# Query-state product over four array tiles, and a written engine order for the first sixteen steps

## The chip, the core and the metric

The kernel runs on one core of one Trainium2 chip. The core has a matrix engine (TensorE, PE in the profile; the loads of its stationary operand are PEld), VectorE (DVE), ScalarE (ACT), GpSimd (POOL) and a queue engine that issues transfers (SP). The metric is the device time of one launch in microseconds (us).

## The reference

Three layers in a row. The first is a delta-rule attention with batch 4, 8 heads, 768 tokens and head size 48; the second a dense two-layer net (384 to 2048 to 384, leaky relu) on the 3072 resulting tokens; the third a layer of 8 experts (384 to 1024 to 384, relu) in which each token goes to one expert.

```
k_n = k / (norm(k) + 1e-6)
for t in range(768):                      # per batch and head
    y[t] = q[t] @ state                   # state: 48 x 48
    state += beta[t] * outer(k_n[t], v[t] - k_n[t] @ state)
h = y @ w_in;  x = max(0.01 * h, h) @ w_out
e = argmax(x @ w_gate)                    # expert of the token
out = prob * sigmoid(x @ w_output_gate)[e] * (relu(x @ w1[e]) @ w2[e])
```

## The kernel before

The 768 tokens are cut into 12 chunks of 64 (`NCH`, `CH`). The 32 batch-head pairs are held 2 x 16: a slot 0 to 15 in the free dimension, and one of the two halves of the partitions (0 to 63, 64 to 127). In a chunk the recurrence is solved with matmuls. The gram of the keys (`gram`, L73) gives a 64 x 64 matrix per head; its diagonal 32 x 32 blocks are copied out (`k_gram_out`, L104, into `td`), transposed, scaled by key norms and beta (`norms`, L169) and inverted row by row (`inverse`, L218), for two chunks, a pair, at a time. `flipped` (L239) transposes the inverse and `z_make` (L254) copies it to z. Pair 0 is inverted on VectorE, every later pair on GpSimd.

`chain` (L298) is a generator that computes one chunk in sections, one for each step: the right side from v and the old state (L339), `solve` with z, with the off-diagonal block lx, and with z again (L316), the state update (L373 to L379), and the result y. y is the sum of two products, both written by `read` (L321, matmul at L323): the query-state product (`state_part`, L347: queries of the chunk times old state) and the masked query-key product ap times the solved u (L384 to L386). `take` (L308) copies the solved columns out of the accumulation banks ks, one half on ScalarE, one on VectorE. y goes to xx as two float16 parts.

The array takes 64 x 64 tiles: the row half follows from the partitions of the operands, the column half from the partitions of the output. In `state_part` before, head half `ab` has operands and output at the same half:

```
        for m in range(GM):
            for g in parts:
                for ab in gs:
                    k.mark_y = read(g, ab, m, old_w, GM * (g ^ ab) + m, half(ab, 48), t.q, m == 0, False)
```

while the product of ap with u runs over `ALL4`, that is over all four pairs of row half and column half. The call `state_part((1,))` is put off (`k.between`) behind the expert product of the third section's step, `state_part((0,))` behind that of the next.

The dense net runs in steps: 8 for each chunk, `moe1_up` (L508, products L518, relu L525 to L532) and `moe1_down` (L536) of one eighth of the 2048 columns. Its weights come as float32 and are made into two float16 parts by `conv` (L450): three VectorE passes (L459 to L461), two ScalarE copies (L466, L467) and a GpSimd subtraction (L468) for each of 24 blocks of 512 columns. Expert weights are converted in the same way in the background from step 16 on (`back`, L481) and stored to DRAM.

`weave` (L947) sets the order. It loads and prepares pair 0, then runs steps n = 0 to 15: chunk 0's and 1's chains, two conversions per step for n below 8 and one for n from 8 to 15, the dense net of chunk 0 from n = 8, and the generator `prepare(1)` (L949), which makes pair 1's inverse. Up to step 16 a scheduler orders the instructions of each engine, within the given program order, priorities and a few written edges (`issue_after`). From step 16 on (L1104) the order of PE, DVE and ACT is the written one. Accumulation banks are drawn from rings: psA and psS (two buffers each, psS for grams, query products and y), psL (two, for the dense net's products and the conversions) and psO (psO0, psO1, for its sums). `moe1_setup` (L409) loads gate weights and constants; its casts are L415, L416 and L420. The transposes and tables of the expert layer come after the last chunk and are not edited.

Of the kernel before, what the change touches and what calls it, by code (L numbers as in the profile page):

```python
# [86 lines left out]
def k_gram(k, c, td):  # L87
    ga = gram_banks(k, c)
    gram(k, ga, k.chunks[c].kc, k.chunks[c].kc, ALL4)
    k_gram_out(k, c, td, ga)  # L90
# [13 lines left out]
def k_gram_out(k, c, td, ga):  # L104
    V, A = k.nc.vector, k.nc.scalar
    for ab in range(2):
        for s, dst, src in td_blocks(c, td, ga, ab):
            if c < 2 and s:
                k.mark_tv = V.tensor_copy(dst, src)
            else:  # L110
                k.mark_td = A.activation(dst, src, AF.Copy)
    for ab in range(2):
        lx_out(k, c, ga, ab)
# [55 lines left out]
def norms(k, w, td):  # L169
    nc = k.nc  # L170
    V, G = nc.vector, nc.gpsimd
    E = V if w == 0 else G
# [14 lines left out]
    for i in range(3):  # L187
        E.tensor_tensor(z, y, y, op=ALU.mult)
        if w:
            E.tensor_tensor(z, z, n2, op=ALU.mult)  # L190
            E.tensor_scalar(z, z, -0.5, 1.5, op0=ALU.mult, op1=ALU.add)
            E.tensor_tensor(y, z, y, op=ALU.mult)
        else:
            V.scalar_tensor_tensor(z, z, -0.5, n2, op0=ALU.mult, op1=ALU.mult)
            V.scalar_tensor_tensor(y, z, 1.5, y, op0=ALU.add, op1=ALU.mult)
    E.tensor_tensor(y, y, n2, op=ALU.mult)
    E.tensor_scalar(y, y, 1e-6, None, op0=ALU.add)
    V.reciprocal(z, y)
    E.tensor_tensor(z, z, z, op=ALU.mult)
    E.tensor_tensor(z, z, k.beta[:, w], op=ALU.mult)  # L200
    E.tensor_scalar(n2, z, -1.0, None, op0=ALU.mult)
    E.tensor_tensor(x, x, n2.unsqueeze(1).to_broadcast([128, 32, 32]), op=ALU.mult)
    if w:
        E.affine_select(x, x, pattern=[[1, 32], [-1, 32]], compare_op=ALU.is_gt, fill=0.0, base=0, channel_multiplier=0)
    E.memset(xf[:, 0:1024:33], 1.0)
    V.transpose(s.nw, y)
    return s
# [63 lines left out]
def q_products(k, c):  # L271
# [4 lines left out]

    def mask():
        for ab in range(2):
            k.nc.vector.tensor_tensor(t.ap[:, GM * ab : GM * ab + GM], gq[ab], k.amask[:, ab : ab + 1].to_broadcast([128, GM, 64]), op=ALU.mult)
# [18 lines left out]
def chain(k, c):  # L298
# [9 lines left out]
    def take(dst, scale):  # L308
        k.mark_uh = A.activation(dst[:, ms[0]], ks[0], AF.Copy, scale=scale)  # L309
        k.mark_u = V.tensor_scalar(dst[:, ms[1]], ks[1], scale, None, op0=ALU.mult)  # L310
# [30 lines left out]
    yield  # L341
    solve(t.z, r, 0, 0, True)
    take(u, 1.0)
    yield
    y = []

    def state_part(parts):  # L347
        if not y:
            y.extend(banks())
        for m in range(GM):  # L350
            for g in parts:
                for ab in gs:
                    k.mark_y = read(g, ab, m, old_w, GM * (g ^ ab) + m, half(ab, 48), t.q, m == 0, False)
# [55 lines left out]
def moe1_setup(k):  # L409
    nc, sb = k.nc, k.const  # L410
    V, A, G = nc.vector, nc.scalar, nc.gpsimd
    k.wg = [sb.tile([128, 3, 16], F16, name=f"wg{h}") for h in range(2)]
    wg32 = sb.tile([128, 3, 16], F32, name="wg32")
    nc.sync.dma_start(wg32, k.wg_d.rearrange("p (a e) -> p a e", a=3))
    A.activation(k.wg[0], wg32, AF.Copy, scale=1024.0)  # L415
    V.scalar_tensor_tensor(k.wg[1], wg32, 1024.0, k.wg[0], op0=ALU.mult, op1=ALU.subtract)  # L416
# [3 lines left out]
    V.tensor_copy(k.cmat, cst)  # L420
# [5 lines left out]
    V.tensor_copy(k.run, k.base)  # L426
# [5 lines left out]
    nc.sync.dma_start(k.xd[DUM : DUM + 1, :], dum)  # L432

# [5 lines left out]
def conv_load(k, pool, n):  # L439
# [4 lines left out]
    else:  # L444
        raw = pool.tile([128, 1024], I32, tag="w64", name=f"w64_{n}")
# [4 lines left out]
def conv(k, pool, n):  # L450
    nc = k.nc
    V, A, G = nc.vector, nc.scalar, nc.gpsimd
    i, which = n // 2, n % 2
    dst, sc = ((k.win, 1024.0), (k.wout, 2048.0))[which]
    w64 = k.w64.pop(n)
    ps, tag = (k.psO, f"psO{n // 2 % 2}") if n < 8 and n % 2 else (k.psL, "psL")
    wt = ps.tile([128, 512], I32, tag=tag, name=f"wt_{n}")
    lo, hi = w64[:, :, 0], w64[:, :, 1]
    V.tensor_scalar(wt, hi, 5, 2, op0=ALU.logical_shift_left, op1=ALU.logical_shift_right)  # L459
    V.scalar_tensor_tensor(wt, hi, -0x40000000, wt, op0=ALU.bitwise_and, op1=ALU.bitwise_or)  # L460
    V.scalar_tensor_tensor(wt, lo, 29, wt, op0=ALU.logical_shift_right, op1=ALU.bitwise_or)  # L461
    w32 = wt.bitcast(F32)
    cs = slice(512 * i, 512 * i + 512)
    h, l = (columns(d)[:, cs] for d in dst)
    ws = pool.tile([128, 512], F32, tag="wt", name=f"ws_{n}")
    A.activation(ws, w32, AF.Copy, scale=sc)  # L466
    A.activation(h, ws, AF.Copy)  # L467
    G.tensor_tensor(l, ws, h, op=ALU.subtract)  # L468
# [478 lines left out]
def weave(k):  # L947
    nc = k.nc
    def prepare(w):  # L949
        a, b = 2 * w, 2 * w + 1  # L950
        td = k.xp.tile([128, 32, 32], F32, tag="xx", name=f"td{w}")
        yield
        yield
        k_gram(k, a, td)
        yield
        yield
        yield
        k_gram(k, b, td)
        yield
        yield  # L960
        with k.tc.high_priority():
            s = norms(k, w, td)
        yield
        for i in range(6):
            inverse(k, w, s, CUTS[i], CUTS[i + 1])
            if i == 5:
                nv_load(k, a)
            yield
        done = k.after
        with k.tc.issue_after(done.ins):  # L970
            nv_make(k, a, s)
        nv_load(k, b)
        yield
        with k.tc.issue_after(done.ins):
            nv_make(k, b, s)
        with k.tc.issue_after(k.mark_gl.ins) if hasattr(k, "mark_gl") else ExitStack():
            flipped(k, w, s)
        z_make(k, a, s)
        yield
        z_make(k, b, s)  # L980

# [11 lines left out]
    k_load(k, 2)  # L993
    q_load(k, 0)
    nv_load(k, 0)
    es = ExitStack()
    wst = es.enter_context(k.tc.tile_pool(name="wst", bufs=2))
    conv_load(k, wst, 0)
    conv_load(k, wst, 1)
    nconv, nback = 0, 0  # L1000
    td = k.p1.tile([128, 32, 32], F32, tag="td", name="td0")
    for c in range(2):
        ga = gram_banks(k, c)
        for s in range(2):
            gram(k, ga, k.chunks[c].kc, k.chunks[c].kc, ((0, s), (1, s)))
        k_gram_out(k, c, td, ga)
    mark_td = k.mark_td
    s0 = norms(k, 0, td)
    masked_scale(k, s0)
    nv_make(k, 0, s0)  # L1010
    inverse(k, 0, s0, 1, 31)
    moe1_setup(k)
    ch = chain(k, 0)
    run(ch)
    run(ch)
    z_make(k, 0, s0, True)
    after = k.after
    turn = nc.gpsimd.tensor_copy(k.const.tile([128, 1], F32, name="turn"), k.z[0][:, 15, 31:32])

    def convert():  # L1020
        nonlocal nconv, es
        if nconv < 24:
            conv(k, wst, nconv)
            ahead = nconv + (10 if nconv < 2 else 6 if nconv < 12 else 2)
            if (nconv < 2 or nconv >= 6) and not 12 <= nconv < 16 and ahead < 24:
                conv_load(k, wst, ahead)
            nconv += 1
            if nconv == 24:
                es.close()
                k.bg = k.late.enter_context(k.tc.tile_pool(name="bg", bufs=6))  # L1030

    k_load(k, 3)
    kg_load(k, 0)
    nv_load(k, 1)
    for n in range(2, 10):
        conv_load(k, wst, n)
    pg = prepare(1)
    hold = ExitStack()
    for m in (mark_td, turn, after):
        hold.enter_context(k.tc.issue_after(m.ins))  # L1040
    for _ in range(4):
        run(pg)
    q_gram(k, 0)
# [345 lines left out]
```

## Time and profile before

| | us |
|---|---|
| median of 3 runs (849.51 to 851.61) | 850.45 |
| the profiled execution, its own time | 855.32 |
| its span, first to last instruction | 853.4 |
| PE busy in the span | 768.0 |
| DVE, ACT, POOL busy in the span | 483.4, 328.6, 414.4 |

The profile is of one execution. An engine is busy while an instruction of it runs; matmuls overlap, so the busy time of a group of them is the union of their spans, and a mean duration is longer than the pace at which they follow. Idle time in brackets stands ahead of an instruction, with what ended it. The granted clock (PEclk) is a share of 2.4 GHz: 0.50 is the lower of its two levels, 1.00 the upper.

### The profile page before, as it was taken

To read this page: it belongs to the slowest core of one execution; us is meant where nothing else is said; L and a number is where in the kernel's file an instruction comes from. 1 tells how busy PE (TensorE), PEld (TensorE's weight loads), DVE (VectorE), ACT (ScalarE), POOL (GpSimd) and SP (SyncE) were. 2 spreads that over 40 slices of the span, in tenths; PEclk is the share of its full clock that TensorE was granted. 3 is DMA by queue.
4 is the path that set the end of the run, shared out by engine and by line. 5 is a ranking of instruction groups with operands and counts; after the bars stand their busy time and mean duration, and the time that the engine had idled before them with its cause. 6 is when DMAs were issued, how large, how long until landed. Compare 5 with 4: busy or idle time off the path is not lost. (4 is left out here: it accounts for less than half of the span.)

```text
span 853.4 us, 29444 instructions
## 1 busy us (share of the span) xinstructions
PE 768.0 (90%) x12642; PEld 591.4 (69%) x12642; DVE 483.4 (57%) x1109; ACT 328.6 (39%) x650; POOL 414.4 (49%) x590
## 2 busy tenths in 40 slices
PE   4044898999999999999999999999997999999993
PEld 4044676777777777777777777777775778778782
DVE  2999784766666566657666767775362222222230
ACT  2246546434644464445534465543311111111110
POOL 0017995688468846884588526521132221222110
PEclk7555799999999999999999999999998999999997
DMA  8714434724662458244724397948726537898440
GB/s 265 269 51 148 153 108 142 183 82 142 194 205 71 138 183 228 73 139 144 216 81 139 121 271 214 319 142 323 326 69 221 84 85 214 223 337 232 134 115 13
DMA packets 100137, 145.03 MB, mean 170 GB/s; under 512 B 42320, under 2 KB 69747, under 8 KB 97186
## 3 DMA queue, kind: packets, MB, share of 16 engines
q1 hardware_dynamic: 94882, 128.10, 49.5%
q0 software_dynamic: 5120, 15.00, 5.7%
q8 instruction: 101, 1.65, 0.8%
q14 instruction: 34, 0.28, 0.1%
HBM read 152.28 MB, written 35.42 MB: 220 GB/s over the span
## 5 line engine op out<-in xcount | busy, mean ns | idle before, releaser
L518 PE MATMUL h<-xx,win 128*128 128x256 f16 x1728 | 207.1, 275 | 1.4 <-ACT ws L466 1.4
L543 PE MATMUL o<-wout,gh 128*128 128x384 f16 x768 | 186.0, 326 | 0.7 <-ACT u L309 0.6
L518 PEld LDWEIGHTS <-win 128*128 128x128 f16 x1728 | 164.5, 98 | 27.7 <-issue 1.4
L543 PE MATMUL o<-wout,gl 128*128 128x384 f16 x384 | 123.6, 326 | 2.5 <-DVE gl L532 2.5
L888 PEld LDWEIGHTS <-wb 128*128 128x128 f16 x2016 | 115.7, 98 | 4.8 <-issue 1.4
L528 DVE SCALAR_TENSOR_TENSOR h<-h,g 128x512 f32<-128x512 f32 x96 | 66.7, 695 | 72.1 <-ACT g L525 67.8
L525 ACT ACTIVATE g<-h 128x512 f32<-128x512 f32 x96 | 57.3, 597 | 122.6 <-PE h L518 114.2
L888 PE MATMUL hp<-xT,wb 128*128 128x128 f16 x1728 | 100.9, 220 | 0.0
L892 DVE SCALAR_TENSOR_TENSOR h<-hp,h 128x512 f16<-128x512 f32 x48 | 33.2, 692 | 118.8 <-ACT h L891 108.8
L543 PEld LDWEIGHTS <-gh 128*128 128x128 f16 x768 | 70.8, 98 | 42.7 <-issue 0.8
L491 POOL TENSOR_SCALAR we<-we 128x512 f32<-128x512 f32 x35 | 52.8, 1510 | 97.8 <-ACT whl L487 78.2
L532 DVE TENSOR_TENSOR gl<-h,gh 128x512 f16<-128x512 f32 x96 | 66.3, 690 | 58.1 <-ACT gh L529 56.9
L902 PE MATMUL o<-wb,h 128*128 128x384 f16 x576 | 97.4, 326 | 0.0
L908 POOL DMA_INDIRECT out_dram<-y,row x24 | 23.9, 998 | 141.5 <-DVE y L907 135.5
L529 ACT ACTIVATE gh<-h 128x512 f16<-128x512 f32 x96 | 57.3, 597 | 85.6 <-DVE h L528 85.5
L891 ACT ACTIVATE h<-hp 128x512 f16<-128x512 f32 x48 | 28.7, 597 | 157.8 <-PE hp L888 157.8
L232 POOL TENSOR_TENSOR x<-x,tmp 128x30 f32<-128x30 f32 (+9 forms) x150 | 81.3, 542 | 11.2
L230 POOL TENSOR_TENSOR tmp<-x 128x30 f32<-128x30 f32 (+9 forms) x150 | 77.9, 519 | 10.8
L902 PEld LDWEIGHTS <-h 128*128 128x128 f16 x576 | 55.3, 98 | 34.4
L487 ACT ACTIVATE whl<-we 128x512 f16<-128x512 f32 x96 | 56.6, 623 | 6.8 <-DMA we<-in_we_dram 3.5
L316 PE MATMUL ks<-r,z 32*32 32x48 f32 x1536 | 27.6, 212 | 35.0 <-DVE z L259 28.2
L494 DVE SCALAR_TENSOR_TENSOR whl<-we,whl 128x512 f16<-128x512 f32 x61 | 51.9, 869 | 10.9 <-ACT whl L487 9.2
(253 smaller groups left out, 1018.3 us busy)
## 6 DMA issues: line engine op xcount, KB each, us to landing
wb<-wd SPq DMA_DIRECT2D x56, 1536.0 KB
we<-in_we_dram SPq DMA_DIRECT2D x96, 256.0 KB
wd<-whl SPq DMA_DIRECT2D x96, 256.0 KB
kc<-in_kt_dram SPq DMA_DIRECT2D x24, 224.0 KB
q<-in_qt_dram SPq DMA_DIRECT2D x24, 224.0 KB
nv<-in_kv_dram SPq DMA_DIRECT2D x12, 384.0 KB
kn<-in_kv_dram SPq DMA_DIRECT2D x12, 384.0 KB
w<-in_win_dram SPq DMA_DIRECT2D x6, 512.0 KB
```

The lines of the kernel that those rows point to most:

```text
L230: E.tensor_tensor(tv, x[:, q, j : j + 1].to_broadcast([128, n, j]), x[:, j : j + 1, 0:j].to_broadcast([128, n, j]), op=ALU.mult)
L232: k.after = E.tensor_tensor(x[:, q, 0:j], x[:, q, 0:j], tv, op=ALU.add)
L487: nc.scalar.activation(hl[:, 0], w32, AF.Copy, scale=sc)
L491: nc.gpsimd.tensor_scalar(w32, w32, sc, None, op0=ALU.mult)
L518: PE.matmul(hp[:, ff], k.win[l][:, f, kk], xx[:, r, kk], start=(n == 0), stop=(n == 8))
L525: A.activation(g32, hp, AF.Copy, scale=0.01 * 2.0**-10)
L528: V.scalar_tensor_tensor(hp, hp, 2.0**-10, g32, op0=ALU.mult, op1=ALU.max)
L529: k.mark = A.activation(gh, hp, AF.Copy)
L532: k.mark_gl = V.tensor_tensor(gl, hp, gh, op=ALU.subtract)
L543: k.mark_down = k.nc.tensor.matmul(k.o[t], gg[l][:, ff, 128 * t : 128 * t + 128], k.wout[r][:, f], start=(f == 0 and i == 0), stop=(f == N ...
L888: PE.matmul(hp[:, ff], w1[:, l, kk, 128 * f : 128 * f + 128], t.xT[:, 3 * r + kk], start=(i == 0), stop=(i == 8))
L902: nc.tensor.matmul(o, t.h[l][:, f], w2[:, r, f], start=(i == 0), stop=(i == 23))
```

## The change

Half of the heads (those in slots with `b1` = 1) get their keys, queries and state at the other partition half than their result: `layout_attention` permutes them on the host, and `read` takes the column half p and the rows separately. Four consecutive calls of `state_part` then go over both row halves and both column halves, and its two calls move: for odd chunks the first is put behind the expert product of the step of the first solve, for even chunks it stands in the chain ahead of the lx solve; the second always follows the second z solve.

Up to step 16 all four engines follow a written order now. Copies of the grams of chunks 0 and 1 come ahead of the casts of constants; `moe1_setup` is split into loads (`moe1_loads`), casts, and `gate_weights` in step 14. The grams of chunks 2 and 3 are written before pair 0's inverse. Loads are issued in another order. Conversions become a stream of single passes (`Conv`): `take` and the end of the sections call `k.fill`, which writes the next ones; 7 blocks come before the first expert product, the others in the eight steps of chunk 0. For the first six blocks the low part is made by TensorE: a bank is opened with an identity product, VectorE writes the value into it, and a product with a negated scaled identity subtracts the high part. Pair 1's inverse is cut by rows: 12 after chunk 0, then three in each step.

```
 def gram_banks(k, c):
-    ps, tags = (k.psO, ("psO0", "psO1")) if c in (1, 2) else (k.psS, ("psS", "psS"))
+    ps, tags = (k.psO, ("psO0", "psO1")) if c in (1, 3) else (k.psL, ("psL", "psL")) if c == 2 else (k.psS, ("psS", "psS"))
...
     def take(dst, scale):
+        k.fill()
         k.mark_uh = A.activation(dst[:, ms[0]], ks[0], AF.Copy, scale=scale)
...
-    def read(g, ab, m, w, f, p, right, clear, last):
+    def read(g, p, m, w, f, rows, right, clear, last):
         cols = 64 if c == 0 or w is old_w else 48
-        return PE.matmul(y[g][half(ab, cols), m % NPR, m // NPR], w[p, f * D : f * D + cols], right[p, f], start=clear, stop=last, skip_group_check=True)
+        return PE.matmul(y[g][half(p, cols), m % NPR, m // NPR], w[rows, f * D : f * D + cols], right[rows, f], start=clear, stop=last, skip_group_check=True)
...
+    def state_part(part):
+        if not y:
+            y.extend(banks())
+        for i in range(NPR):
+            for b in gs:
+                g, m = b ^ 1 ^ part, NPR * b + i
+                for p in gs:
+                    read(g, p, m, old_w, GM * (g ^ p) + m, half(p ^ b, 48), t.q, part == 0 and i == 0, False)
+
     solve(t.z, r, 0, 0, True)
     take(u, 1.0)
+    if c > 1 and c % 2:
+        k.between.append(lambda: state_part(0))
     yield
...
+    if c > 1 and c % 2 == 0:
+        state_part(0)
     solve(t.lx, u, 0, 1, False)
     take(r, -1.0)
-    if c > 1:
-        k.between.append(lambda: state_part((1,)))
     yield
     if c == 1:
-        state_part(gs)
-    with k.tc.issue_after(k.mark_y.ins) if c == 1 else ExitStack():
-        solve(t.z, r, 1, 1, True)
+        state_part(0)
+    solve(t.z, r, 1, 1, True)
     if c > 1:
-        k.between.append(lambda: state_part((0,)))
+        k.between.append(lambda: state_part(1))
     take(u, 1.0)
     yield
...
                 f = GM * ab + m
                 PE.matmul(ks[s][half(ab, 48), m], t.kg[half(s), f], u[half(s), f], start=True, stop=True, skip_group_check=True)
+        k.fill()
+        if c == 1:
+            state_part(1)
...
         for ab, s in ALL4:
-            read(s ^ ab, ab, m, u_w, GM * ab + m, half(s), t.ap, c == 0, True)
+            p = ab ^ (m // NPR)
+            read(s ^ p, p, m, u_w, GM * ab + m, half(s), t.ap, c == 0, True)
+    k.fill()
...
+def conv_bank(k, ps, tag, name):
+    wt = ps.tile([128, 512], I32, tag=tag, name=name)
+    k.nc.tensor.matmul(wt.bitcast(F32), k.ident, k.ident.unsqueeze(1).to_broadcast([128, 4, 128]), start=True, stop=True)
+    return wt
...
+    def low(self):
+        if self.bank is not None:
+            self.k.nc.tensor.matmul(self.w32, self.k.minus[:, self.n % 2], self.h, start=False, stop=True, skip_group_check=True)
+            self.k.nc.scalar.activation(self.l, self.w32, AF.Copy, scale=self.sc)
...
+    nv_load(k, 0)
+    wg32, cst = moe1_loads(k)
     q_load(k, 0)
-    nv_load(k, 0)
+    k_load(k, 3)
...
+    order = es.enter_context(k.tc.manual_schedule(engines={E.PE, E.DVE, E.Activation, E.Pool}))
...
+    ga = k_gram(k, 3)
+    k_gram_out(k, 3, td, ga)
+    banks = [conv_bank(k, k.psO, f"psO{i}", f"wb{i}") for i in range(2)] + [conv_bank(k, k.psL, "psL", f"wc{i}") for i in range(2)]
+    inverse(k, 0, s0, 1, 31)
     z_make(k, 0, s0, True)
...
+    fills += [
+        [lambda: pair.update({1: norms_first(k, 1, td)}), vec],
+        [mask, vec],
+        [vec, vec],
+        [lambda: norms_second(k, 1, pair[1]), vec],
+        [vec],
+    ]
...
+    for n in range(8, 16):
+        s = n - 8
         down, up = up, None
...
+        moe1_up(k, 0, s, (lambda: ops(BEFORE[s]), lambda: ops(1)))
+        up = (0, s, k.gg)
+        sca()
+        inv(1)
+        for _ in range(AFTER[s]):
+            ops(3)
+            sca()
+        if s == 0:
+            q_products(k, 1)()
+        if s < 6:
+            run(ch)
...
+        sca()
+        inv(2)
...
         if s == 7:
-            ch = chain(k, p + 1)
+            ch = chain(k, 2)
             run(ch)
...
+            ga = k_gram(k, 4)
+            k_gram_out(k, 4, td, ga)
+            flipped(k, 1, pair[1])
+            z_make(k, 2, pair[1])
+            z_make(k, 3, pair[1])
...
+EARLY = 6
+BEFORE = (2, 2, 2, 2, 2, 2, 2, 2)
+HOMES = "010101010SSLLLLLLLAAAALL"
+AFTER = (1, 2, 2, 2, 1, 1, 1, 0)
...
     for s, h, ab, b1, pr in np.ndindex(2, 2, 2, 2, NPR):
-        at = 2 * (s ^ ab) + b1, 2 * pr + ab
+        p = ab ^ b1
+        at = 2 * (s ^ p) + b1, 2 * pr + p
```

## Rows read from the trace of the kernel before

**Rows 1.** Busy time by stage: start:end, length, busy (instructions) per engine, clock, DMA.
```profile
core 0: us, PE busy (x) PEld busy (x) DVE busy (x) ACT busy (x) POOL busy (x), PEclk, DMA share, GB/s
27.00:50.00 23.00, 0.00 (x0) 0.00 (x0) 22.58 (x119) 2.86 (x9) 1.19 (x1) 0.50 0.48 151
50.00:92.00 42.00, 23.09 (x594) 20.55 (x595) 41.86 (x71) 26.43 (x51) 25.37 (x37) 0.54 0.39 134
92.00:135.00 43.00, 43.00 (x722) 31.02 (x722) 30.55 (x48) 22.55 (x42) 39.39 (x66) 0.94 0.33 107
...
150.00:350.00 200.00, 197.84 (x3804) 149.86 (x3805) 131.44 (x284) 96.34 (x202) 143.25 (x233) 1.00 0.52 152
350.00:558.00 208.00, 205.98 (x3887) 155.30 (x3880) 139.76 (x283) 104.56 (x204) 134.45 (x176) 1.00 0.61 181
```

**Rows 2.** Busy time by stage, two stretches of 10 us, same columns.
```profile
80.00:90.00 10.00, 6.34 (x166) 5.78 (x164) 9.96 (x20) 5.26 (x9) 8.44 (x14) 0.50 0.51 173
130.00:140.00 10.00, 7.72 (x163) 5.88 (x161) 3.07 (x5) 4.35 (x11) 7.23 (x14) 1.00 0.41 137
```

**Rows 3.** Timeline, 0 to 51 us: start, length, engine, line, out<-in [idle before <-releaser].
```profile
3.82 5.38 PE L77 MATMUL ga<-kc 48*64 48x64 f32 x128 [3.82 <-DMA kc<-in_kt_dram]
...
15.76 0.24 ACT L415 ACTIVATE wg<-wg 128x48 f16<-128x48 f32 x1 [5.62 <-DMA wg<-in_wg_dram]
...
17.27 1.76 DVE L109 COPY td<-ga 32x256 f32<-32x256 f32 x4
...
19.07 1.25 DVE L180 STREAM_TRANSPOSE x<-td 128x1024 f32<-128x1024 f32 x1
...
23.99 1.03 DVE L332 SCALAR_TENSOR_TENSOR ks<-nv,nw 128x384 f32<-128x384 f32 x2
...
27.13 1.07 DVE L230 TENSOR_TENSOR tmp<-x 128x14 f32<-128x14 f32 x1
...
49.91 0.37 DVE L259 COPY z<-zt 128x256 f32<-128x256 f32 x1
...
50.34 2.47 PE L316 MATMUL ks<-r,z 32*32 32x48 f32 x64 [28.23 <-DVE z L259]
```

**Rows 4.** Timeline, 80 to 165 us, TensorE and VectorE.
```profile
91.76 4.00 PE L518 MATMUL h<-xx,win 128*128 128x256 f16 x18 [1.41 <-ACT ws L466]
...
135.26 2.14 PE L518 MATMUL h<-xx,win 128*128 128x256 f16 x18
...
138.13 1.25 DVE L241 STREAM_TRANSPOSE zt<-x 128x1024 f32<-128x1024 f32 x1 [5.05 <-POOL x L234]
...
142.97 0.88 PE L316 MATMUL ks<-r,z 32*32 32x48 f32 x64 [1.17 <-ACT r L309]
...
149.00 0.88 PE L316 MATMUL ks<-u,lx 32*32 32x48 f32 x64
...
152.47 1.15 PE L323 MATMUL y<-q,state 48*64 48x64 f32 x32 [0.51 <-ACT td L120]
```

**Rows 5.** Groups by line, 50 to 135 us: busy, mean ns | idle before, releaser.
```profile
L459 DVE TENSOR_SCALAR wt<-w 128x512 int32<-128x512 int32 x12 | 8.2, 689 | 1.0 <-ACT ws L466 0.9
L528 DVE SCALAR_TENSOR_TENSOR h<-h,g 128x512 f32<-128x512 f32 x8 | 5.6, 696 | 4.6 <-ACT g L525 4.6
...
L468 POOL TENSOR_TENSOR win<-ws,win 128x512 f16<-128x512 f32 x12 | 13.9, 1157 | 14.3 <-ACT win L467 14.3
```

**Rows 6.** Timeline of TensorE: both products of y, each with the instruction behind it.
```profile
117.65 1.10 PE L323 MATMUL y<-ap,u 64*48 64x64 f32 x60
118.68 2.14 PE L518 MATMUL h<-xx,win 128*128 128x256 f16 x18
...
158.49 1.15 PE L323 MATMUL y<-q,state 48*64 48x64 f32 x32
159.57 0.50 PE L543 MATMUL o<-wout,gh 128*128 128x384 f16 x2
```

More of the change, by code (lines that the diff above doesn't have):

```diff
@@ L169, in norms @@
 def norms(k, w, td):
[L170 to L172 removed]
+    V = k.nc.vector
     s = Ctx()
@@ L444, in conv_load @@
     else:
-        raw = pool.tile([128, 1024], I32, tag="w64", name=f"w64_{n}")
+        raw = pool.tile([128, 1024], I32, tag="w64", bufs=3, name=f"w64_{n}")
     k.nc.sync.dma_start(raw, (k.win_d, k.wout_d)[which][i].bitcast(I32))
     k.w64[n] = raw.rearrange("p (a b) -> p a b", b=2)
[L450 to L468, printed above, removed]
@@ L948, in weave @@
     nc = k.nc
[L949 to L980, printed above, removed]
     def run(g):
@@ new lines, in weave, with fill, stream @@
+    q_load(k, 1)
+    for n in range(6, 10):
+        conv_load(k, k.wst, n)
+    kg_load(k, 1)
+    nback = 0
+    E = mybir.EngineType
+    order = es.enter_context(k.tc.manual_schedule(engines={E.PE, E.DVE, E.Activation, E.Pool}))
+    ready, fills = [], []
+    def fill():
+        for f in fills.pop(0) if fills else ():
+            f()
+    k.fill = fill
+    def stream():
+        homes = dict(zip("01SLA", ((k.psO, "psO0"), (k.psO, "psO1"), (k.psS, "psS"), (k.psL, "psL"), (k.psA, "psA"))))
+        for n, home in zip(ORDER, HOMES):
+            u = Conv(k, n, banks[n % 4] if n < EARLY else None, homes[home])
+            for _ in u.vector():
+                yield
+            ready.append(u)
+            yield
@@ L1001, in weave, with ops, vec, inv @@
+    late = []
+    todo = stream()
+    def ops(n):
+        for _ in range(n):
+            next(todo, None)
+    def vec():
+        ops(3)
+    rows = iter(range(1, 31))
+    def inv(n):
+        for j in [j for _, j in zip(range(n), rows)]:
+            inverse(k, 1, pair[1], j, j + 1)
+    def sca():
+        for u in ready:
+            u.scalar()
+            late.append(u)
+        ready.clear()
+    def low():
+        for u in late:
+            u.low()
+        late.clear()
     td = k.p1.tile([128, 32, 32], F32, tag="td", name="td0")
+    gas = []
@@ L1002, in weave @@
     for c in range(2):
-        ga = gram_banks(k, c)
+        gas.append(gram_banks(k, c))
         for s in range(2):
-            gram(k, ga, k.chunks[c].kc, k.chunks[c].kc, ((0, s), (1, s)))
-        k_gram_out(k, c, td, ga)
-    mark_td = k.mark_td
-    s0 = norms(k, 0, td)
+            gram(k, gas[c], k.chunks[c].kc, k.chunks[c].kc, ((0, s), (1, s)))
+    for c in range(2):
+        td_out(k, c, td, gas[c])
+    for c in range(2):
+        for ab in range(2):
+            lx_out(k, c, gas[c], ab)
@@ L1009, in weave @@
+    s0 = norms(k, 0, td)
+    nc.scalar.activation(k.cmat, cst, AF.Copy)
+    nc.scalar.activation(k.wg[0], wg32, AF.Copy, scale=1024.0)
+    k.minus = k.const.tile([128, 2, 128], F16, name="minus")
+    for w in range(2):
+        nc.scalar.activation(k.minus[:, w], k.ident, AF.Copy, scale=-(2.0 ** -(10 + w)))
+    ga = k_gram(k, 2)
     masked_scale(k, s0)
+    td = k.p1.tile([128, 32, 32], F32, tag="td", name="td1")
+    k_gram_out(k, 2, td, ga)
     nv_make(k, 0, s0)
-    inverse(k, 0, s0, 1, 31)
@@ L1012, in weave @@
-    moe1_setup(k)
+    nv_make(k, 1, s0)
     ch = chain(k, 0)
@@ L1015, in weave @@
     run(ch)
-    z_make(k, 0, s0, True)
[L1017 to L1043, printed above, removed]
[L1044 to L1070 removed]
+    mask = q_products(k, 0)
@@ new lines, in weave @@
+    run(ch)
+    sca()
+    run(ch)
+    low()
+    sca()
+    z_make(k, 1, s0)
+    run(ch)
+    low()
+    sca()
+    run(ch)
+    low()
+    sca()
+    run(ch)
+    low()
+    sca()
+    inv(12)
+    ch = chain(k, 1)
+    run(ch)
+    low()
+    banks.clear()
+    ops(3)
+    run(ch)
+    sca()
+    up = down = tail = None
+    for n in range(8, 16):
+        s = n - 8
+        down, up = up, None
+        moe1_up(k, 0, s, (lambda: ops(BEFORE[s]), lambda: ops(1)))
+        up = (0, s, k.gg)
+        sca()
+        inv(1)
+        for _ in range(AFTER[s]):
+            ops(3)
+            sca()
+        if s == 0:
+            q_products(k, 1)()
+        if s < 6:
+            run(ch)
+        if s == 5:
+            k_load(k, 5)
+        sca()
+        inv(2)
@@ L1082, in weave @@
+            z_make(k, 2, pair[1])
+            z_make(k, 3, pair[1])
+        if s == 1:
+            k_load(k, 4)
+        if s in (2, 3):
+            nv_load(k, s)
+            nv_make(k, s, pair[1])
+        if s == 3:
+            q_load(k, 2)
+        if s == 5:
+            kg_load(k, 2)
+        if s == 6:
+            gate_weights(k, wg32)
         if down is not None:
             moe1_down(k, *down)
-            if down[1] == 7:
-                tail = moe1_tail(k, down[0], k.o)
-        with k.tc.issue_after(k.mark_down.ins) if down is not None else ExitStack():
-            if n and n not in (1, 3, 15):
-                run(pg)
-            if n == 12:
-                td = k.p1.tile([128, 32, 32], F32, tag="td", name="td2")
-            if n == 13:
-                k_load(k, 5)
@@ L1093, in weave @@
-    hold.close()
+    es.close()
+    k.bg = k.late.enter_context(k.tc.tile_pool(name="bg", bufs=6))
     for n in range(AHEAD):
```

157 lines of the change are left out of this document (80 added, 77 removed).

## The prediction

> **What bounds the kernel now.** I began with the busy time by stage [rows 1]. From 150 to 558 us TensorE is busy 403.8 of 408 us at full clock: there, whatever shortens TensorE's list shortens the kernel. From 92 to 135 it is busy throughout, but up to 92 it is not the bound: no matmul from 27 to 50, 23.1 of 42 us from 50 to 92 at clock 0.54, while VectorE is busy 22.6 of 23 and 41.9 of 42. From 558 on nothing is edited. The page's chain of work that ended last reaches back only over the final stores, so the early bound has to come from the order of time.
>
> The timeline of the start [rows 3] shows VectorE's serial path. The first grams run from 3.82 to 9.20, but chunk 1's copies come only at 17.27, because ScalarE stood 5.62 us before a cast of gate weights whose load had not landed. The transpose follows at 19.07, the row-by-row inverse at 27.13, z at 50.28, and TensorE's solve, after 28.23 us without work, at 50.34.
>
> The second path is seen in the steps [rows 4]. The first expert product starts at 91.76, step 16 at 135.26. VectorE's flip of pair 1's inverse (138.13 to 139.38) waited 5.05 us for GpSimd, and the solve of chunk 2 runs at 142.97. Behind that TensorE is dense.
>
> **The change, part by part.** Sums are against the profiled execution: span 853.4, its own time 855.32, which is 4.87 above the median 850.45. I take 4.87 off at the end.
>
> *Start.* Gate-weight and constant casts go behind the copies of chunks 0 and 1. The grams end at 9.20; ScalarE's copies follow at once and VectorE's some 0.8 later, at about 10.1 in place of 17.27: 7.2 earlier. Norms, the two subtractions of 1.03 us and one take still stand ahead of the inverse [rows 3], which takes as long as before, so z comes at about 43.3. The SP queue issues nv 0 and the constants ahead of q 0, k 3 and the weight loads. DMA engines are half idle from 27 to 50 [rows 1], and the delayed loads are wanted after 43, so I cost them at nothing; if q 0 were late, its mask would only trade places with a conversion. Bounds of this part: 5.6 (the wait alone) and 8.
>
> *z to the flip.* In both kernels VectorE has 24 conversions of three passes here, each pass 0.69 us [rows 5], besides takes, masks, norms and relu. Before, from 50 to the flip's end at 139.4, it was busy 41.9 + 30.6 + 1.3 (the flip) = 73.8 us, and idle the rest. The new order starts products after some 7 conversions in place of 16 and spreads the others over the eight steps, so the same work can run without the late wait. Its floor is 43.3 + 73.8 = 117.1. Seven conversions of 2.1 us and some 8 us of takes, mask, norms, state and xx bring VectorE from 43.3 to about 66, where the first product starts. I add: 1.2 for the masks of chunk 2 that move in; 3 for conversions now written as three dependent passes (about 0.12 us more each over the back-to-back pace, in those that were interleaved before); 2.3 for the first relu, whose product takes 4.00 at low clock [rows 4] and a ScalarE copy behind it 0.6, while two filler passes take VectorE only to 68.3; 1.8 for other waits on ScalarE in eight steps (such waits were 4.6 in eight relus [rows 5]). The flip ends at 125.4, 14.0 earlier. From there to chunk 2's solve it was 3.6; two of the copies that stood in it now stand ahead of it, so 2.8. **The ramp gains 14.8.** Bounds: 23 if VectorE only meets its floor; 0 if each of eight steps waits for ScalarE or GpSimd by about 1.8 us more.
>
> GpSimd must not become later than that. It was busy 25.4 + 39.4 us from 50 to 135 [rows 1], with 24 low-part subtractions of 1.157 us [rows 5]. Six leave it (6.9 us), becoming six matmuls with a negated identity and six ScalarE copies. The rest, about 60 us, starts near 45 and waits some 7 for VectorE's second norm part: the inverse ends around 112 to 117, ahead of the flip by 5 or more. The ten added matmuls (four that open the banks, six subtractions, 512 columns each) cost at most 0.44 apiece by the cold row (4.00/18 for 256 columns), 4.4 in all, in a stretch where TensorE was idle 45%: nothing. TensorE's own work in the eight steps is about the 43 us of the 92 to 135 stretch, less than VectorE's 56.
>
> *Query-state product.* A part is 16 calls, recorded as 32 matmuls, and takes 1.08 us from its start to the next instruction's [rows 6]: 34 ns each, two of the four 64 x 64 tiles of the array at work. With half the heads' keys and state at the other partition half, consecutive calls go to all four tiles, as in the product of ap with u, whose 60 matmuls take 1.03, 17 ns each [rows 6]. So a part becomes 0.55, saving 0.53. Chunks 2 to 11 have two parts each in the dense stretch: 20 x 0.53 = **10.6**. Bounds: 0 (the pace stays) and 10.8.
>
> Here a rule bears on the sum. In the ap-with-u row, the first two calls of four come from different row halves and write the same bank at different partitions, just as the changed calls do; its pace is 17 ns. The Trainium skill (TensorEngine Tiling (Array Packing), Restrictions and Gotchas) says that different row tiles cannot access one PSUM bank at the same time; by that the parts would keep their pace and this term be 0 instead of 10.6. The row speaks against it.
>
> *Where the parts stand.* For odd chunks the first part goes one step earlier; for even ones it stands directly ahead of the lx solve, and it needs both psS banks. In later chunks these were emptied a step before. In chunk 2 they hold the gram of chunk 5: the lx solve ran at 149.00, but that gram's copies ended only at 152.4 (the part at 152.47 still waited 0.51 for them [rows 4]). Now the wait falls on TensorE with the solve, the take behind it and the next product queued behind: up to 3.4 lost, 0 if the copies come sooner. I take **2.5** lost, nearer the row.
>
> Sum: 855.32 - 14.8 - 10.6 + 2.5 = 832.4 in a profile, less 4.87: **828 us**.
>
> **The rivals.**
>
> *The row halves take turns.* If two row halves writing one bank exclude each other, the parts stay at 1.08: 850.45 - 14.8 + 2.5 = 838. For it: grams keep each row half to its own bank. Against: the ap-with-u pace [rows 6]. Chance 0.08.
>
> *A new wait takes the old one's place in the ramp.* Four engines now run in one written order; conversions share psL with the products and only two ws buffers stand between ScalarE and GpSimd. If each step waits some 1.8 us more, the ramp gains nothing and only the tiles count: 850.45 - 10.6 + 2.5 = 842. For it: the waits of 4.6 us at relu [rows 5]. Against: filler passes are written around each relu. Chance 0.12.
>
> *TensorE's clock stays low in the eight steps* (slower). They start near 66 rather than 92, and TensorE has gaps since VectorE sets the pace. Half clock makes 43 us of work 86: step 16 then starts at 152 in place of 135.3, 16.7 later; less the 3.5 us of waits that stood before chunk 2's solve, less 10.6, plus 2.5: 850.45 + 5.1 = 855.6. It decides once the steps take over 81 us, a mean clock of about 0.53. For it: 80 to 90 us, TensorE busy 63% at clock 0.50. Against: 130 to 140, busy 77% and still 1.00 [rows 2]; 43/56 is 77%. Chance 0.05.
>
> That the change is not what it says: the tile order is plain in the calls, so a pace other than those two would surprise me.
>
> **How the numbers follow.** Forecast 0.71, at 828; its own terms give 817 (850.45 - 23 - 10.6, VectorE at its floor and no bank wait) to 835 (850.45 - 8.8 - 10.6 + 3.4, six of the ramp's fifteen us lost and the full bank wait). The two rivals at 838 and 842 still count as faster, each partly inside the range; some 0.03 is left around no change, where both lose together. A measurement of this kernel can tell about 0.3%, 2.6 us, from no change. Faster 0.91, same 0.03, slower 0.06 (the clock, and a little for a mishap in the ramp beyond it). Range 816 to 841: from just under the floor case to most of both rivals.
>
> **What would show it.** Right: chunk 1's copies on VectorE near 10, z near 43, first expert product near 66 (it was 91.76), the flip's end near 125 and chunk 2's solve near 128; 32-matmul state parts at about 0.55 from start to next; TensorE dense from there to the end of the attention, and the stage from 558 on as long as before. A wait of 2 to 3 us before chunk 2's first state part would show the bank term. Wrong: parts still at 1.08 (first rival); waits at psL or ws that stretch the eight steps beyond 60 us (second); a clock near 0.5 in them (third).

## The result and the profile after

The changed kernel takes 837.10 us (median of 4 runs, 834.92 to 839.83), the kernel before 849.98 beside it (4 runs): ratio 0.9853, 95% interval 0.9813 to 0.9893. Forecast were 828.0 in a range of 816 to 841. It is faster, by 12.9 of the 22 us forecast. The profiled execution took 837.97, its span is 835.7. The two profiled executions lie 17.4 us apart (855.32 - 837.97), 4.5 more than the medians, and the stage tables below are of these two. Lines of the changed kernel lie higher: `solve` is L321, `state_part`'s matmul L328, the expert product L556, relu L566.

Busy time by stage of the kernel after, columns as in [rows 1]:

```profile
43.80:131.90 88.10, 64.72 (x1263) 45.21 (x1264) 74.56 (x121) 47.44 (x86) 61.49 (x100) 0.88 0.35 114
66.00:92.00 26.00, 18.73 (x366) 12.95 (x364) 20.34 (x33) 12.63 (x22) 24.12 (x36) 0.82 0.48 158
92.00:135.00 43.00, 34.74 (x530) 24.75 (x530) 33.44 (x54) 26.44 (x49) 25.43 (x37) 0.88 0.38 124
150.00:160.00 10.00, 10.00 (x154) 6.40 (x155) 4.48 (x8) 3.91 (x7) 2.72 (x11) 0.83 0.48 147
150.00:350.00 200.00, 199.03 (x3842) 148.74 (x3839) 128.23 (x282) 95.58 (x197) 146.33 (x236) 0.99 0.50 146
```

The same view of the kernel before, from its z to its flip's end:

```profile
50.30:139.40 89.10, 68.81 (x1340) 53.65 (x1340) 73.38 (x119) 49.92 (x95) 67.54 (x106) 0.76 0.38 128
```

From z to the flip's end VectorE did 74.6 us of work in 88.1, before 73.4 in 89.1: the stretch begins 6.5 us earlier and is hardly shorter. In the steps the mean clock was 0.82 and 0.88, against 0.50 in [rows 2]'s first line.

The timeline after, in the order of [rows 3] and [rows 4]:

```profile
10.56 1.76 DVE L108 COPY td<-ga 32x256 f32<-32x256 f32 x4 [0.93 <-ACT td L110]
12.36 1.25 DVE L181 STREAM_TRANSPOSE x<-td 128x1024 f32<-128x1024 f32 x1
...
43.42 0.38 DVE L253 COPY z<-zt 128x256 f32<-128x256 f32 x1
44.12 1.50 PE L321 MATMUL ks<-r,z 32*32 32x48 f32 x64 [16.16 <-ACT z L252]
65.64 0.82 PE L556 MATMUL h<-xx,win 128*128 128x256 f16 x3 [0.62 <-DMA xx<-xx]
66.94 0.82 PE L556 MATMUL h<-xx,win 128*128 128x256 f16 x3 [0.48 <-DMA xx<-xx]
68.16 2.74 PE L556 MATMUL h<-xx,win 128*128 128x256 f16 x12 [0.40 <-DMA xx<-xx]
71.57 0.70 DVE L566 SCALAR_TENSOR_TENSOR h<-h,g 128x512 f32<-128x512 f32 x1 [3.90 <-ACT g L563]
...
123.31 1.91 POOL L228 TENSOR_TENSOR x<-x,nz 128x1024 f32<-128x1024 f32 x1
130.65 1.24 DVE L235 STREAM_TRANSPOSE zt<-x 128x1024 f32<-128x1024 f32 x1
131.87 2.14 PE L556 MATMUL h<-xx,win 128*128 128x256 f16 x18
134.53 0.49 ACT L311 ACTIVATE r<-ks 128x384 f32<-128x384 f32 x1
135.89 0.88 PE L321 MATMUL ks<-r,z 32*32 32x48 f32 x64
136.70 2.14 PE L556 MATMUL h<-xx,win 128*128 128x256 f16 x18
138.77 1.16 PE L77 MATMUL ga<-kc 48*64 48x64 f32 x64
139.87 0.50 PE L581 MATMUL o<-wout,gh 128*128 128x384 f16 x2
...
144.59 0.33 PE L328 MATMUL y<-q,state 48*64 48x64 f32 x4 [2.60 <-ACT td L123]
145.08 0.68 PE L328 MATMUL y<-q,state 48*64 48x64 f32 x28 [0.16 <-DVE td L128]
145.69 0.88 PE L321 MATMUL ks<-u,lx 32*32 32x48 f32 x64
146.51 1.26 PE L556 MATMUL h<-xx,win 128*128 128x256 f16 x10
149.73 1.15 PE L556 MATMUL h<-xx,win 128*128 128x256 f16 x8 [1.96 <-issue]
...
157.21 0.69 PE L328 MATMUL y<-q,state 48*64 48x64 f32 x32
157.84 0.50 PE L581 MATMUL o<-wout,gh 128*128 128x384 f16 x2
```

The start came as forecast: copies at 10.56, z at 43.4 to 43.8, first product at 65.64. The flip no longer waits for GpSimd (its last row ends at 125.2), but comes at 130.65. Chunk 2's solve is at 135.89 against 142.97 [rows 4]: 7.1 gained, not 14.8. At 144.59 the bank wait stands, 2.60 and 0.16, and the product behind it is broken in two by 1.96 us that the trace puts down to no releaser. A part takes 0.63 to the next instruction (157.84 - 157.21), against 1.08 [rows 6].

TensorE's groups by shape in the dense stretch, 165 to 575 us, in the kernel before:

```profile
L323 PE MATMUL y<-q,state 48*64 48x64 f32 x576 | 20.7, 221 | 0.0
```

and after:

```profile
L328 PE MATMUL y<-q,state 48*64 48x64 f32 x576 | 13.5, 225 | 0.9 <-ACT td L123 0.9
```

One matmul lasts as long as before (225 ns against 221), but the 576 cover 13.5 us of the engine in place of 20.7: more of them overlap.

Where the lead comes and goes is seen in the start of ScalarE's first relu copy of each step, in us:

| step | 8 | 12 | 16 | 17 | 18 | 20 | 40 | 103 |
|---|---|---|---|---|---|---|---|---|
| before | 96.5 | 115.8 | 142.8 | 147.3 | 153.5 | 164.7 | 272.5 | 603.7 |
| after | 70.9 | 105.4 | 134.9 | 139.4 | 151.0 | 163.3 | 268.2 | 589.0 |
| lead | 25.6 | 10.4 | 7.9 | 7.9 | 2.5 | 1.4 | 4.3 | 14.7 |

Step 8 starts 25.6 us earlier and the eight steps give 17.7 of it back; conversions now lie between them. From step 17 to 20 all but 1.4 us of the rest is lost. From 20 to 103 the lead grows by 13.3. The last 3.0 (17.7 in the span) come where nothing was edited; they are counted as no part of the change.

### The profile page after: what moved, and what is told of

It is laid out like the page before. It is cut to its first block, busy times and chain, and to the rows that moved or that the text cites. A ratio compares the mean times of both kernels' runs of the same rounds, so it can differ in the third digit from the quotient of the medians.

```text
span 835.7 us, 29458 instructions
## 1 busy us (share of the span) xinstructions
PE 757.3 (91%) x12652; PEld 577.0 (69%) x12652; DVE 479.6 (57%) x1108; ACT 330.4 (40%) x653; POOL 408.2 (49%) x584
## 5 line engine op out<-in xcount | busy, mean ns | idle before, releaser
L556 PE MATMUL h<-xx,win 128*128 128x256 f16 x1728 | 211.9, 278 | 12.3 <-ACT ws L497 4.6
L556 PEld LDWEIGHTS <-win 128*128 128x128 f16 x1728 | 166.5, 99 | 42.1 <-issue 7.2
L581 PE MATMUL o<-wout,gh 128*128 128x384 f16 x768 | 188.4, 329 | 0.9 <-ACT gh L567 0.8
L566 DVE SCALAR_TENSOR_TENSOR h<-h,g 128x512 f32<-128x512 f32 x96 | 66.7, 695 | 77.5 <-ACT g L563 77.0
L226 POOL TENSOR_TENSOR x<-x,tmp 128x30 f32<-128x30 f32 (+9 forms) x150 | 81.3, 542 | 11.6
L581 PEld LDWEIGHTS <-gl 128*128 128x128 f16 x384 | 37.7, 98 | 26.5 <-DVE gl L570 1.5
```

The lines of the kernel that those rows point to most:

```text
L226: k.after = E.tensor_tensor(x[:, q, 0:j], x[:, q, 0:j], tv, op=ALU.add)
L556: PE.matmul(hp[:, ff], k.win[l][:, f, kk], xx[:, r, kk], start=(n == 0), stop=(n == 8))
L566: V.scalar_tensor_tensor(hp, hp, 2.0**-10, g32, op0=ALU.mult, op1=ALU.max)
L581: k.mark_down = k.nc.tensor.matmul(k.o[t], gg[l][:, ff, 128 * t : 128 * t + 128], k.wout[r][:, f], start=(f == 0 and i == 0), stop=(f == N ...
```

## Experiments

They ran in three batches: e1 to e4; r_after (the changed kernel itself again), e5, e6, e7; and e5 again with e8, e9, e10. The kernel before had medians of 857.71, 855.84 and 857.78 us in them. The batches ran on two chips and before's medians lie above the 849.98 of the first measurement, so only ratios, and times within a batch, are compared. The changed kernel had 0.9907 in the second batch.

**r_after.** The changed kernel, unedited, as the base of its batch.

> The changed kernel itself, for comparison on the chip of the runs beside it: ratio to the kernel before near 0.985.

Ratio 0.9907 [0.9885, 0.9929], 847.68 us. Its steps 17 and 18 stand at 138.3 and 150.0, 11.7 apart (after 11.6, before 6.2), so the loss between these steps repeats.

**e1: the parts on two tiles again**, all else as changed.

```
-        for i in range(NPR):
-            for b in gs:
+        for b in gs:
+            for i in range(NPR):
```

> The changed kernel with the calls of each state part in another order only: the bank half b outermost, so that consecutive calls use two of the four array tiles again. Theory A (most of the gain is the tiles, in the dense stretch): 32 matmuls take about 1.08 us again in place of 0.61, 20 parts cost 9.4, time about 846.5. Theory B (the tiles only feed waits elsewhere, the written order carries the gain): parts take 1.08, but the time rises by 4 or less, to about 841. If the pace stays at 0.61, both are wrong about what sets it.

0.9916 [0.9891, 0.9941], 850.96. The edit did not restore the old pace: parts take 0.91, some 1.14 to 1.23, not 1.08; the layout alone gave some of it. The 20 parts take 19.5 us, in r_after 15.9, and against r_after's 0.9907 the time can't be told apart. The intervals are too wide to say whether these 3.6 us count; that they do not show asked where they are lost.

**e2: tiles without the written order.** The new placement of heads in the kernel before, its order to step 16 kept; parts stand in the chain where the changed kernel has them.

```
-                    k.mark_y = read(g, ab, m, old_w, GM * (g ^ ab) + m, half(ab, 48), t.q, m == 0, False)
+                    k.mark_y = read(g, p, m, old_w, GM * (g ^ p) + m, half(p ^ b, 48), t.q, part == 0 and i == 0, False)
...
+    if c > 1 and c % 2 == 0:
+        state_part(0)
     solve(t.lx, u, 0, 1, False)
```

> The kernel before with the new placement of heads, the four-tile state parts and their new positions in the chain, but the old order and conversions up to step 16. Theory A: 850.0 - 9.5 = 840.5, so that the written order is worth about 3. Theory B: about 846, the order worth 9.

1.0022 [1.0010, 1.0034], 859.66: no gain at all, rather a small loss. TensorE's waits from 140 to 600 us (us in total, times, longest):

```profile
PE y L323 <- ACT td L120: 4.0, 4, 3.4
```

The first part of chunk 2 waits 3.4 here, step 18 starts at 160.9 in place of before's 153.5. That the place of the even chunks' parts can cost what the tiles bring is a guess here; e9, which differs from e2 in that place, tests it.

**e3: gram of chunk 5 one step earlier**, so that the banks are free when chunk 2's part wants them.

```
-            c = a if odd and s == 5 else p + 3 if not odd and s == 0 and p > 2 else 5 if n == 17 else NCH
+            c = a if odd and s == 5 else p + 3 if not odd and s == 0 and p > 2 else 5 if n == 16 else NCH
```

> The changed kernel with the gram of chunk 5 in step 16 rather than 17, so that both psS banks are empty when chunk 2's first state part stands ahead of its lx solve. Theory A: the wait of 2.6 us ahead of that part goes, and with it part of the slower clock behind it: 837.1 - 3 to 5 = 832 to 834. Rival: the copies of that gram only lengthen step 16, where ScalarE already does the gram of chunk 4 and z of two chunks: within 1 us of 837.1, with a wait of about the same size ahead of chunk 2's first solve.

0.9867 [0.9846, 0.9888], 846.79. The wait is gone (timeline of e3, TensorE):

```profile
143.01 0.69 PE L328 MATMUL y<-q,state 48*64 48x64 f32 x32
143.63 0.88 PE L321 MATMUL ks<-u,lx 32*32 32x48 f32 x64
144.45 2.14 PE L556 MATMUL h<-xx,win 128*128 128x256 f16 x18
```

The product behind it is whole, and step 18 starts at 146.7, against 150.7 in e1 on the same chip, where it waits. The rival has a share, too: from step 16 to 17 it takes 6.7 us, in e1 4.5. The interval only just touches that of r_after, so e3 alone does not settle the size.

**e4: late conversions staged in SBUF**, not in the products' bank group psL.

```
-HOMES = "010101010SSLLLLLLLAAAALL"
+HOMES = "010101010SSBBBBBBBAAAABB"
```

(B is the SBUF pool `k.wst`.)

> The changed kernel with nine of the conversions (those staged in psL) staged in SBUF, so that psL is left to the products of the eight steps. Theory A (the eight steps are long because products wait for a psL buffer until ScalarE has copied a conversion, and relu waits behind them): the waits of products for ScalarE's ws copy and for gl (8.8 us in three) go, the flip's end moves from 131.9 to about 126, time 837.1 - 4 = 833. Rival (VectorE's list or GpSimd sets the pace): the flip's end stays within 2 us, time within 1.5 us of 837.1; if passes that write SBUF collide with GpSimd, they get longer than 0.69 and the flip later.

0.9941 [0.9921, 0.9961], 852.87, slower than the changed kernel. VectorE's groups from 64 to 135 us, in the changed kernel:

```profile
L484 DVE SCALAR_TENSOR_TENSOR wt<-w,wt 128x512 int32<-128x512 int32 x10 | 7.0, 696 | 0.3
```

and in e4, where the group mixes passes that write SBUF with passes that write a bank:

```profile
L484 DVE SCALAR_TENSOR_TENSOR wt<-w,wt 128x512 int32<-128x512 int32 x10 | 9.0, 898 | 0.3
```

Single passes of e4's timeline, the first two staged in SBUF, the third in a bank:

```profile
86.92 1.52 DVE L484 SCALAR_TENSOR_TENSOR wt<-win,wt 128x512 int32<-128x512 int32 x1
88.97 1.04 DVE L486 SCALAR_TENSOR_TENSOR wt<-win,wt 128x512 int32<-128x512 int32 x1
108.03 0.70 DVE L484 SCALAR_TENSOR_TENSOR wt<-w,wt 128x512 int32<-128x512 int32 x1
```

From 83 to 106 us the 14 second and third passes staged in SBUF take 0.91 to 1.53 us instead of 0.70, and the flip ends later, at 134.65 (131.84 in e1 on the same chip). The cure cost more than the wait. The waits of the expert products for ws and gl are gone in e4, and still its eight relus wait 5.9 us (7.5 in the changed kernel). From z to the flip's end VectorE is idle 10.4 us and busy 80.7, in e1 13.6 and 74.5. So psL is a part of what holds the steps up, some 3 us at most, and not the whole.

**e5: the even chunks' parts behind the expert product, too.** Both use `k.between` now; the first comes after the lx solve's step, the second after the state update's. Odd chunks stay.

```
-    if c > 1 and c % 2 == 0:
-        state_part(0)
     solve(t.lx, u, 0, 1, False)
     take(r, -1.0)
+    if c > 1 and c % 2 == 0:
+        k.between.append(lambda: state_part(0))
...
-    if c > 1:
+    if c > 1 and c % 2:
         k.between.append(lambda: state_part(1))
...
             state_part(1)
+        elif c % 2 == 0 and c > 1:
+            k.between.append(lambda: state_part(1))
```

> The changed kernel; for even chunks the first state part goes back behind the expert product of the step of the lx solve, and the second to that of the state update. Theory C (for even chunks the tiles' gain is given back, because a part that fills both psS banks at once now waits for ScalarE's copies of the second half of a gram): the part of chunk 2 no longer waits 2.6 us, those of chunks 4, 6, 8, 10 take 0.63 in place of 1.40, together 2.8 + 3.1 us and some of the slow clock behind the first: 5 to 8 us faster than the changed kernel of this batch. Rival (TensorE would only wait elsewhere in those steps): within 2 us of it.

0.9827 [0.9809, 0.9845], 840.68: 7.0 us below r_after's 847.68 in the same batch, and faster than both kernels. From step 17 to 18 it takes 6.5 us in place of 11.7, so 5.2 of the 7.0 come there. All 20 parts take 0.63 (sum 12.5, in r_after 15.9).

What those parts waited for in later chunks shows in the timeline of the kernel after, chunk 6, TensorE with ScalarE's copies:

```profile
317.42 0.41 ACT L94 ACTIVATE lx<-ga 128x256 f32<-128x256 f32 x1
317.68 1.52 ACT L123 ACTIVATE td<-ga 32x256 f32<-32x256 f32 x4
...
318.46 0.33 PE L328 MATMUL y<-q,state 48*64 48x64 f32 x4
319.25 0.68 PE L328 MATMUL y<-q,state 48*64 48x64 f32 x28 [0.46 <-ACT td L123]
```

The first four matmuls go to the bank already emptied, the rest wait for ScalarE's copies of the gram, which end at 319.20. This repeats at chunks 4, 6 and 8: their first parts take 1.16, 1.40 and 1.16 in the kernel after, 1.8 us more than 0.63 in all. Chunk 10's takes 0.62, so the 3.1 expected for four chunks was too much.

**e6: e5 and e3 together.**

> The same, and the gram of chunk 5 in step 16 as in the earlier run. Theory C: the two edits remove the same wait of chunk 2, so within 1.5 us of the run before. Rival (the early gram has a gain of its own, by taking ScalarE's copies out of step 17): 2 or more faster than that run.

0.9834 [0.9817, 0.9852], 840.97, the same as e5: both edits remove the same wait.

**e7: third VectorE pass left out** in conversions 7 to 23.

```
-        V.scalar_tensor_tensor(wt, lo, 29, wt, op0=ALU.logical_shift_right, op1=ALU.bitwise_or)
+        if n < 7:
+            V.scalar_tensor_tensor(wt, lo, 29, wt, op0=ALU.logical_shift_right, op1=ALU.bitwise_or)
```

> The changed kernel without the third pass (the lowest three bits of the weight) of conversions 7 to 23: it leaves out 17 VectorE passes of 0.69 us in the eight steps, 12 us. Theory A1 (VectorE's list sets the eight steps): the flip's end comes 9 to 12 us earlier, at about 121, and the time falls by as much less what GpSimd's inverse (done at 125.2) then holds: at least 6. Rival A2 (the products are held by psL and ScalarE's copies, relu by the products): the idle time ahead of relu grows by the passes left out, the flip moves by under 4.

0.9813 [0.9791, 0.9835], 839.65: 8.0 below r_after. The flip in r_after's timeline:

```profile
129.53 1.24 DVE L235 STREAM_TRANSPOSE zt<-x 128x1024 f32<-128x1024 f32 x1
```

and in e7's:

```profile
123.01 1.24 DVE L235 STREAM_TRANSPOSE zt<-x 128x1024 f32<-128x1024 f32 x1
```

17 passes of 0.69 are 11.7 us, the flip moved by 6.5, 1.0 of it because z already came earlier in this execution. So about half of VectorE's list passes through to the flip and the other half only gives way to waits (each step's second float16 part now waits 0.66 us for ScalarE, which the left-out pass had filled). It lies between the two theories. The median falls by 8.0, so what the flip gains does reach the end of the kernel.

**e8: GpSimd's inverse spread over the steps**, on e5: `inv(12)` becomes `inv(7)`, `inv(1)` in each step `inv(2)`. In the changed kernel ScalarE's copy waits 3.16 us for the GpSimd queue at the start of the steps.

> That version with 7 rows of pair 1's inverse ahead of the first product in place of 12, and 4 rows in each step in place of 3. In the changed kernel ScalarE stands 3.16 us before a ws copy in the first of the eight steps, because GpSimd first finishes 12 rows, and the take behind it holds TensorE for 3.2. Theory D (written order on GpSimd delays ScalarE): that wait falls below 1, the flip's end comes 2 to 3 us earlier, and the time falls by about 2. Rival (VectorE's list holds the steps anyway): flip within 1 us, time within 1 us of the version without it.

0.9827 [0.9812, 0.9842], 842.54, beside e5 again at 842.95. That wait is gone, but the flip starts at 129.62 instead of 130.18 and the time can't be told from e5's: this wait for GpSimd was not what held the ramp.

**e5 again**, as the base of the third batch.

> The version with the even chunks' parts behind the products, again, as the reference of this batch: ratio to the kernel before 0.983 as it was.

0.9842 [0.9826, 0.9858], 842.95.

**e9: tiles alone, parts placed as in e5.** e2 with e5's edit, order to step 16 as before.

> The kernel before, with its old order and conversions up to step 16, with the new placement of heads and four-tile parts, but the even chunks' parts behind the products. Theory C (the tiles' gain was hidden by waits for the psS banks): 20 parts x 0.45 = 9 us faster than the kernel before, ratio 0.989; the rest of the version's gain, about 0.6%, is then the written order. Rival (the four tiles bring little even with no wait, the written order everything): ratio 0.996 or more.

0.9946 [0.9928, 0.9964], 852.15. Without the written order, tiles and places are worth 857.78 - 852.15 = 5.6 us; in e2, with the even chunks' parts at the other place, it was nothing. No run parts the tiles from the moved places in these 5.6. The written order on top of it is worth 852.15 - 842.95 = 9.2.

**e10: e5 with the two-tile order of e1**, now with no wait that could hide the pace.

> The version with the even chunks' parts behind the products, with the bank half outermost, so that consecutive calls use two tiles; no part waits for banks in either. Theory C: a part takes about 0.92 in place of 0.63, 20 parts cost 6 us, ratio 0.990 if the version is at 0.983. Rival (time saved in a part is lost again in the step): within 2 us of the version.

0.9853 [0.9837, 0.9869], 843.80, only 0.9 above e5, and the intervals overlap. TensorE's groups by shape, 165 to 575 us, in e5 again:

```profile
L321 PE MATMUL ks<-r,z 32*32 32x48 f32 x1152 | 17.9, 203 | 2.0 <-issue 1.8
L328 PE MATMUL y<-q,state 48*64 48x64 f32 x576 | 12.5, 224 | 0.0
```

and in e10:

```profile
L328 PE MATMUL y<-q,state 48*64 48x64 f32 x576 | 17.6, 224 | 0.0
L321 PE MATMUL ks<-r,z 32*32 32x48 f32 x1152 | 16.8, 203 | 0.6 <-issue 0.6
```

The parts give up 5.1 us, but the z solves shrink by 1.1 and stand idle 1.4 less. That leaves 2.6 of the 5.1, and step 103 does start 2.5 later in e10's profile (589.0, in e5 again 586.5). One such place, a solve in e5 again's timeline:

```profile
275.46 0.69 PE L321 MATMUL ks<-r,z 32*32 32x48 f32 x42
276.43 0.47 PE L321 MATMUL ks<-r,z 32*32 32x48 f32 x22 [0.28 <-issue]
276.83 2.14 PE L558 MATMUL h<-xx,win 128*128 128x256 f16 x18
```

and the same solve in e10's:

```profile
276.56 0.88 PE L321 MATMUL ks<-r,z 32*32 32x48 f32 x64
277.37 2.14 PE L558 MATMUL h<-xx,win 128*128 128x256 f16 x18
```

With four tiles the solve breaks and takes 1.37 us to the next instruction instead of 0.81: 0.56, twice the 0.28 that a part is faster. Steps 40 to 48, with two parts in them, take 42.8 us in e5 and in e10 alike, and in every other profile of the three batches. The place is a fixed one: in all ten profiles of these batches with four tiles the z solve of the steps 26, 42, 58 and 74 stands idle 0.22 to 0.33 us, in the two with two tiles (e1, e10) it does not. The two profiles of the first measurement, before on two tiles and after on four, do not show it there. What holds TensorE the trace does not name ("issue"), and such idle time as a whole is not tied to four tiles: over 160 to 600 us the solves of r_after lost 2.7 us to it, those of the first changed profile 0.3, and of the kernel before, on two tiles, 1.9. No run took it away with four tiles kept; its cause stays open.

## Why the prediction was right in direction and too large in size

**Start: right.** Forecast were chunk 1's copies 7.2 earlier and z at 43.3; the copies came 6.7 earlier and z at 43.8.

**z to the flip: the failed term.** Forecast 82.1 us to the flip's end at 125.4, measured 88.1 to 131.9. VectorE's work was right: 74.6 against 73.8 and 1.2 of masks. Its idle time was 88.1 - 74.6 = 13.5 where the allowance left 7.1. The term that failed is "1.8 for other waits on ScalarE in eight steps", which measured 6.9 (relus 3.6, xx 2.2, gl 0.7, ws 0.5), and with it the 2.3 for the first relu, which measured 3.9. A load took 0.6, and the gaps between passes 2.1 instead of 3. VectorE's relu from 64 to 135 us in the changed kernel, against 4.6 in [rows 5]:

```profile
L566 DVE SCALAR_TENSOR_TENSOR h<-h,g 128x512 f32<-128x512 f32 x8 | 5.6, 699 | 7.6 <-ACT g L563 7.5
```

and, in us in total, times and longest, VectorE's waits before xx and TensorE's before the expert product:

```profile
DVE xx L402 <- ACT xx L401: 2.2, 2, 1.9
PE h L556 <- ACT ws L497: 4.6, 2, 2.4
PE h L556 <- DVE gl L570: 4.2, 1, 4.2
```

The first relu's 3.9 is its product: it ran at a clock of 0.50 (66 to 72 us), waited 0.88 for the transfers of xx, and ended at 70.90, 5.26 after its start where 4.00 was taken. Later products wait 8.8 for a bank that a conversion or the last step's result still holds. That is the second rival's mechanism, and the ramp lost about half of that rival's price. By e4 these bank waits are some 3 of the 13.5 at most; e7 shows list and waits in equal parts; e8 clears the wait for GpSimd. What sets the rest, ScalarE's list or the order of the dependent steps, stays open. GpSimd's inverse ended at 125.2 where 112 to 117 was forecast, ahead of the flip by 5 all the same.

Between flip and solve it took 4.0, not 2.8. The copies did not hold it: the last, of r, ended at 135.02, but TensorE had the step's expert product and the sums behind it in its list, without idle time from 131.87 to the solve at 135.89. Together the ramp gave 7.1 of the 14.8.

**The bank wait: its size right, its consequences not.** 2.5 was taken, 2.76 measured. But "in later chunks these were emptied a step before" was wrong: chunks 4, 6 and 8 wait for the same copies (e5's section). And what is queued behind the wait costs more than the wait: the broken product's 1.96, then 150 to 160 us at a clock of 0.83, where TensorE had been idle. Step 17 to 18 lost 7.9 - 2.5 = 5.4 us. E5 is 7.0 faster by the place of the parts alone, 5.2 of them in this step.

**Tiles: the pace right, its worth not.** Parts went from 1.08 to 0.63, 0.08 short of the 0.55 taken. The first rival is out: the parts did not stay at 1.08. The grams, in which each row half writes a bank of its own, go at 17 ns (64 in 1.10 us, from 138.77 to 139.87), the product of ap with u, in which both write one, at 17 too [rows 6], and the new parts at 20. So sharing a bank costs a call little. The Trainium skill (TensorEngine Tiling (Array Packing), Restrictions and Gotchas) has different row tiles unable to access one PSUM bank at once; these paces speak against it for writes to different partitions of the bank. One thing is not parted: in the kernel before all calls of a part write one bank, in the new order they go to two banks in turn, so four tiles and two banks came together, and no run had the one without the other. But "there, whatever shortens TensorE's list shortens the kernel" did not hold for the parts: of 10.6 us forecast for their list, the profile after has 6.7 (the 20 parts took 21.6 before and 14.9 after), and e10 against e5 shows that 5.1 us of list are worth 0.9 by the medians and 2.5 by the profiles. A busy share of 99% did not make the engine's list the bound to the last nanosecond.

**The clock: right to doubt its rival.** It was 0.82 and 0.88 in the steps and 0.99 over 150 to 350 us.

In sum, in the profile: forecast 14.8 + 10.6 - 2.5 (of its other sums one is off by rounding: the upper case of its own terms is 834.5, not 835). Found: 7.9 at step 17, 6.5 lost to step 20, 13.3 won in the dense stretch. That last is more than the 6.3 of its 18 parts: the z solves (2.4) and the grams (2.5) of this execution took less of TensorE and had less "issue" idle ahead than before's. R_after's had as much idle as before's or more (2.7 us in the solves and 1.1 in the grams, before 1.9 and 1.1). So part of the first measurement's gain may not repeat, as 0.9907 against 0.9853 suggests; the intervals touch.

The version that beats both kernels is e5: 0.9827 and 0.9842 of before in two batches.

## What to carry to other kernels

Before an operation that needs all buffers of a ring is moved ahead of the work that used to cover it, look in each iteration, not in one, for the last reader of every buffer; the wait costs itself and whatever it breaks behind it. Take the idle time of the engine whose list sets a stage from rows per step, since work that is spread over dependent steps fills fewer gaps than a floor of busy time promises. And a faster burst on an engine that is 99% busy is worth what a run without it shows, not its busy time.

## What the runs showed of the hardware

Four array tiles in turn, two of them writing one PSUM bank from different row halves, ran at 20 ns per 48x64 fp32 matmul, against 34 on two tiles and one bank; the loop order of e10 on the new layout, two tiles at a time, gave 28 (0.91 us). The solves carry idle stretches of 0.2 to 0.5 us with no releaser, between 0.3 and 3.3 us of them in one execution (after and e5), and between the profiles of e10 and e5 they and the longer solves took half of what faster parts had given. An int32 pass of VectorE with two tensor operands took 0.70 us when staged in PSUM; staged in SBUF 14 of 18 took 0.91 to 1.53, the others 0.68 to 2.28 (e4). The one-source pass took 0.69 in PSUM and 0.41 to 0.87 in SBUF. GpSimd was busy beside nearly all of them, so its share in this is not shown.
